# The last output tiles of a two-branch attention kernel: opened ahead on TensorE, closed in two halves, read out by two engines

## The chip, the cores and the metric

The kernel runs on one core of a Trainium2 chip. The metric is the time of one execution in microseconds on the device; of three runs of the kernel before, the median is 965.25 us (964.43 to 966.57). The engines are called as in the profile: PE (matmuls), PEld (its weight loads), DVE and ACT (vector and scalar engine), POOL, and SP, which here only issues transfers. PSUM, where PE writes its results, has eight banks of 128 x 512 f32.

## The reference

Two attention branches share one input x (2048 x 640, bf16) and are mixed by a gate per row:

```python
g = _sigmoid((x * gate_w).sum(-1, keepdims=True))
a = _A_ref(x, A_wqkv, A_wo)      # 32 heads of 20, full softmax attention over 2048 keys
b = _B_ref(x, B_wqkv, B_wo)      # 32 heads of 20, 8 keys at distances 0, 2, ..., 14 back
return g * a + (1 - g) * b
```

Each branch projects x to q, k, v, takes softmax(q k / sqrt(20)) v for each head, and multiplies the heads' results by its own 640 x 640 output matrix (wo).

## The kernel before, in words

**Groups and steps.** Branch A's queries are cut into four chunks of 512 (`QCN`), its heads into eight sets of four (`NQUAD`). One chunk with one set is a group; there are 32, and the chunk is the outer loop. A group has 64 units (16 key blocks x 4 heads). A unit is a score matmul into one PSUM bank, an exponential, and a P·V matmul into bank 5 (`OB`), where each of the four heads has its own 32 partitions. The units are taken in steps of three and two in turn: even steps use banks 0, 1, 2, odd steps banks 3, 4. There are 819 steps, 0 to 818 (`NS`); the last has three units. `mk_qk` (L1061) issues a step's scores, `mk_exp` (L1076) its exponential on ACT into one of six buffers, `mk_pv` (L1084) its P·V matmuls, for several steps together.

**The order.** There is no dynamic scheduling on the chip: the Python program writes one list of instructions per engine, and each engine runs its list in order, waiting on semaphores that `_Sched` derives from the buffers which a task reads and writes. The main loop over steps issues the exponential of step s, then the scores of step s + 2, then whatever side work a small planner finds room for. Side work is written as generators ("lanes": `gen_k`, `gen_q`, `gen_F`, ...), which yield what they need next: `("pe", cost, ...)` for PE time, `("dw", time, cost, ...)` for the DVE work that frees a bank. The planner compares these costs with its own clocks (`lim_pe`, `lim_dve`) and holds a lane back until the step has room for it. Banks 6 and 7 belong to the side work (`take`, `give`). Where there is none, fillers are put on PE (`idle_mm`): into bank 6 or 7 when one is free (L1200), otherwise multiplications by zero added to bank 5 (L1204).

**After a group.** `do_norm` (L629) transposes bank 5 into `rg`, and `gen_norm` takes the reciprocal of the sums (L637), multiplies it by the gate (L638), scales (L643) and transposes back into a slot of `oTn` (L646). All five are on DVE.

**Output.** For a chunk of 512 rows, the output is eight tiles of 128 rows x 320 columns (four blocks `blk`, two halves `hf`). A tile is the sum of 5 matmuls with branch B's result (`b_mm`) and 8 with branch A's (`a_mm`, one per set of heads). `gen_fold` does this for chunks 0 to 2 once the chunk's eight groups are done.

The last chunk is different, since its last group ends with the program. `gen_prefold` computes, while the last two groups run, each tile's sum of B's five matmuls and A's first six (`NPF`), and DVE copies it as f32 into `accin` (L696), which lies in the old weights `WqkB`. After the last P·V matmul, `last_fold` multiplies by the sets six and seven (L708): first eight matmuls of set six, one per tile, into all eight banks, then, after the last group's norm, eight of set seven. DVE then adds `accin` to each bank, tile by tile (L715), into `outl`. After two tiles a block of 128 rows is complete, and a transfer of 160 KB takes it out (L718), on SP and ACT in turn.

Of the kernel before, what the change touches and what calls it, by code (L numbers as in the profile page):

```python
# [5 lines left out]
FP32 = mybir.dt.float32  # L6
# [226 lines left out]
def _build(ctx, nc, A_x, A_wqkv, A_wo, B_wqkv, B_wo, gate_w, out):  # L233
# [69 lines left out]
    lgt = [WqkA[:, 2 + i, D:D + 512] for i in range(2)]  # L303
    repp = [[WqkA[:, 0, D:D + 512], WqkA[:, 1, D:D + 512]], [WkP[i][:, 0:4, :].rearrange("p c k -> p (c k)") for i in range(2)]]
    rep_dead = [[("WkA", 1)], [("WkP", 0), ("WkP", 1)]]
    accin = WqkB[:, :, :].rearrange("p c k -> p (c k)").bitcast(FP32)[:, 0:4 * D].rearrange("p (b k) -> p b k", b=4)
    outl = WvB[:, :, :].rearrange("p c k -> p (c k)")[:, 0:4 * D].rearrange("p (b k) -> p b k", b=4)

    x_v = A_x[0].rearrange("(b p) d -> p b d", p=P)
# [5 lines left out]
    def fap(t, first, dims):  # L315
        return bass.AP(tensor=t, offset=first.offset, ap=[[first.ap[0][0], P]] + dims)
# [123 lines left out]
    def give(b, evac):  # L440
        held[b] = False
        if cur[0] is not None:
            cur[0].hold -= 1
        free_at[b] = evac.fin + 56.0
# [182 lines left out]
    def do_norm(gi):  # L627
        i = gi % 2
        return T("dve", lambda e: e.transpose(rg[i][:, :], bank[OB]), reads=[("ob", j) for j in range(4)],  # L629
                 writes=["rg"], cost=720)  # L630

    def gen_norm(gi):
        qc, q = divmod(gi, NQUAD)
        i = gi % 2
        sl = gi % NOT
        yield ("dve", 420.0, 0.0)
        T("dve", lambda e: e.reciprocal(rr[i][:, :], rg[i][:, 0:512:32]), reads=["rg"], writes=[("rr", i)], cost=240)  # L637
        T("dve", lambda e: e.tensor_tensor(rr[i][:, :], rr[i][:, :], gA[:, 16 * qc:16 * qc + 16], ALU.mult),  # L638
          reads=["gA"], writes=[("rr", i)], cost=180)
        rg_v = fap(rg[i], rg[i][:, 1:2], [[32, 16], [1, DH]])  # L640
        rr_b = fap(rr[i], rr[i][:, 0:1], [[1, 16], [0, DH]])
        yield ("dve", 500.0, 0.0)
        T("dve", lambda e: e.tensor_tensor(rgn[i][:, :, 1:1 + DH], rg_v, rr_b, ALU.mult),  # L643
          reads=["rg", ("rr", i)], writes=["rgn"], cost=500)
        yield ("dve", 710.0, 0.0)
        T("dve", lambda e: e.transpose(oTn[:, sl, :], rgn[i][:, :, :]), reads=["rgn"], writes=[("oTn", sl)], cost=710)  # L646
        normdone[gi] = True
# [8 lines left out]
    def a_mm(o, qc, q, blk, c0):  # L656
        return (o, oTn[:, (qc * NQUAD + q) % NOT, blk * P:(blk + 1) * P], woA_r[:, q, c0:c0 + FW])
# [4 lines left out]
    def a_rd(qc, qs):  # L662
        return [("oTn", (qc * NQUAD + q) % NOT) for q in qs] + [("woA_r", q) for q in qs]
# [20 lines left out]
    def gen_prefold(qc):  # L684

        while not bdone.get(qc) or not all(normdone.get(qc * NQUAD + q) for q in range(NPF)):
            yield ("poll",)
        for blk in range(4):
            for hf in range(2):
                c0 = FW * hf  # L690
                b = yield from take()
                o = bank[b][:, 0:FW]
                mms = [b_mm(o, blk, c0, dp) for dp in range(CN)] + [a_mm(o, qc, q, blk, c0) for q in range(NPF)]
                t = yield from chain(b, mms, b_rd(blk) + a_rd(qc, range(NPF)), cost=140.0)
                yield ("dw", t.fin, 490.0, 0.0)
                give(b, T("dve", lambda e, b=b, blk=blk, c0=c0: e.tensor_copy(accin[:, blk, c0:c0 + FW], bank[b][:, 0:FW]),  # L696
                          reads=[("bk", b)], writes=[("accin", blk, hf), "WqkB"], cost=420))

    def last_fold(qc):
        bs = (0, 1, 2, 3, 4, 6, 7, OB)  # L700
        for q in range(NPF, NQUAD):
            for blk in range(4):
                for hf in range(2):
                    c0 = FW * hf
                    b = bs[2 * blk + hf]
                    o = bank[b][:, 0:FW]
                    wr = [("bk", b)] + ([("ob", j) for j in range(4)] if b == OB else [])
                    T("pe", lambda e, o=o, blk=blk, c0=c0, q=q: e.matmul(o, *a_mm(o, qc, q, blk, c0)[1:], start=(q == NPF),  # L708
                                                                        stop=(q == NQUAD - 1)),
                      reads=a_rd(qc, [q]), **({"writes": wr} if q == NPF else {"accum": wr}), cost=140)  # L710
        for blk in range(4):
            for hf in range(2):
                c0 = FW * hf
                b = bs[2 * blk + hf]
                T("dve", lambda e, b=b, blk=blk, c0=c0: e.tensor_tensor(outl[:, blk, c0:c0 + FW], bank[b][:, 0:FW],  # L715
                                                                  accin[:, blk, c0:c0 + FW], ALU.add),
                  reads=[("bk", b), ("accin", blk, hf)], writes=[("outl", blk), "WvB"], cost=460)
            T("sp" if blk % 2 == 0 else "act", lambda e, blk=blk: e.dma_start(out_v[:, 4 * qc + blk, :], outl[:, blk, :]),  # L718
              reads=[("outl", blk)], writes=[("outd", qc, blk)], dma=True)


    L_flat = fap(L_sb, L_sb[:, 0, 0:1], [[1, 1024]])
# [290 lines left out]
    for h in range(2):  # L1013
        b = QH[h]

        def fn(e, h=h, b=b):
            ins = None
            for j in range(4):
                r = slice(32 * j, 32 * j + 32)
                ins = e.matmul(bank[b][32 * j:32 * j + 1, 0:256], KM[r, 0:1], qabs[r, 256 * h:256 * h + 256], start=False, stop=True,  # L1020
                               skip_group_check=True)
            return ins
# [78 lines left out]
    def lane(gen, name, s0, s1, total, pos=None):  # L1101
        g = _Lane(gen, name, s0, s1, total)
        if pos is None:
            lanes.append(g)
        else:
            lanes.insert(pos, g)
        return g
# [64 lines left out]
    def force(g, s, until=None):  # L1172
        forcing[0] += 1
        n = 0
        while not g.done and not (until is not None and until()):
            if not ready(g, s, INF, INF):
                for o in lanes:
                    if o is not g and not o.done and (o.hold or n > 300):
                        ready(o, s, INF, INF)
            n += 1  # L1180
            assert n < 200000, g.name
        forcing[0] -= 1
# [56 lines left out]
    for s in range(NS):  # L1239
# [49 lines left out]
        def flush(must, old_only=False):  # L1289
            while pend:  # L1290
                s0, i0, un0 = pend[0]
                g0 = un0[0:2]
                if old_only and g0 != (qc, q):
                    return
                obk = sch.bufs[("ob", 0)]
                if un0[2] == 0 and not must and obk[1]:
                    if max(t.fin for t in obk[1]) > clk["pe"] + 150.0:
                        return
                part = []
                while pend and pend[0][0] == s0 and pend[0][2][0:2] == g0:  # L1300
                    _, i1, un1 = pend.pop(0)
                    part.append((i1, un1))
                for (_, un1) in part:
                    key = (un1[1], un1[2] // 3)
                    if key not in vdone:
                        late.append((s, "v") + key)
                        force(vl[un1[1] // 2], s, lambda key=key: key in vdone)

                n0, npv[0] = npv[0], npv[0] + len(part)
                mk_pv(s0, part, (SWITCH if n0 == 0 else 0.0) + MM * (-(-npv[0] // 4) + (-n0 // 4)))  # L1310
                block[0] = False
                if part[-1][1][2] == KBN - 1 and part[-1][1][3] == 3:
                    g1 = g0[0] * NQUAD + g0[1]
                    if g1 == 0 and not vl[0].done:
                        late.append((s, "gate", 0))
                        force(vl[0], s)
                    if g1 >= NOT and not folddone.get((g1 - NOT) // NQUAD):
                        fl = foldl[(g1 - NOT) // NQUAD]
                        late.append((s, "fold", fl.name))
                        force(fl, s)  # L1320
                    do_norm(g1)
                    lane(gen_norm(g1), "norm%d" % g1, s, s + 1, 1.0, 0)

        if gend:
            flush(False, True)
# [29 lines left out]
        if pend and pend[0][0] <= s - NEB + 2:  # L1355
            flush(True)
        pair_side = (pair_side + block[1]) if npv[0] == 0 else 0.0
        while pair_side < FILL * min(3, npend) and clk["pe"] + MM + SWITCH <= lim_pe and s < NS - 2 and npv[0] == 0:
            if not idle_mm():
                break  # L1360
            nidle += 1
            pair_side += MM
# [6 lines left out]
    for g in list(lanes):  # L1369
        late.append((NS, g.name, 0))  # L1370
        force(g, NS)
    last_fold(QCN - 1)
    _INFO["late"] = late
    _INFO["prof"] = prof
    _INFO["ends"] = ends
# [36 lines left out]
```

## Time and profile before

| | |
|---|---|
| median of three runs | 965.25 us (964.43 to 966.57) |
| the profiled execution | 965.52 us |
| its span, first to last instruction | 963.7 us |
| granted TensorE clock, mean | 0.997 |
| last exponential starts | 951.43 us |
| last P·V matmuls start | 953.19 us |
| last group's norm, from first to last instruction | 953.63 to 956.11 us |
| eight additions (L715) | 956.52 to 961.18 us |
| output transfers issued | 957.63 to 961.6 us |

The page gives for each engine its busy time and its share of the span, and the chain of work that ended last. A row of the timeline has the start in us from the span's start, the length, the engine, the line of the kernel, the operation, what it wrote from what it read, the shape, and the count of instructions merged into the row; the bracket tells how long the engine was idle before and what released it. A row of the groups has the busy time in us and the mean of one instruction in ns after the bar, then the idle time before the group. Matmuls overlap, so that several in a row take less than their mean times their count.

### The profile page before, as it was taken

How to read it: one execution, taken by the hardware profiler on the slowest of the kernel's cores; microseconds unless marked ns; L12 is line 12 of the kernel's file. 1: busy time of each engine (PE TensorE's matmuls, PEld its weight loads, DVE VectorE, ACT ScalarE, POOL GpSimd, SP SyncE). 2: the span in 40 equal slices, each digit the busy share in tenths (PEclk: the TensorE clock that was granted, in tenths of full speed). 3: DMA queues.
4: the chain of work that ended last, by engine and by line, in shares of the span. 5: the costliest groups of instructions: out<-in, count | busy, mean ns of one | idle time of the engine just before them, and what ended most of it. 6: DMA issues, size and time to landing. Idle time of an engine off the chain costs nothing.

```text
span 963.7 us, 16441 instructions
## 1 busy us (share of the span) xinstructions
PE 881.2 (91%) x6408; PEld 287.5 (30%) x6408; DVE 570.4 (59%) x1047; ACT 941.6 (98%) x839; POOL 3.1 (0%) x7
## 2 busy tenths in 40 slices
PE   8999999998998899999998989999999998999996
PEld 5333333322222222223322222323222233222332
DVE  5585443445424888762557798355789536987222
ACT  5999999999999999999999999999999999999995
POOL 1000000000000000000000000000000000000000
PEclk9999999999999999999999999999999999999999
DMA  9000000000000000000000000000000000000000
GB/s 311 5 1 21 15 1 1 2 21 14 1 1 1 1 1 1 2 1 7 15 8 1 1 1 1 9 7 7 9 1 1 1 9 15 8 1 1 1 2 28
DMA packets 12032, 12.86 MB, mean 13 GB/s; under 512 B 3380, under 2 KB 11316, under 8 KB 11956
## 3 DMA queue, kind: packets, MB, share of 16 engines
q1 hardware_dynamic: 9700, 11.27, 3.7%
q8 instruction: 53, 0.87, 0.4%
q10 hardware_dynamic: 2256, 0.53, 0.3%
q14 instruction: 23, 0.19, 0.1%
HBM read 9.18 MB, written 2.62 MB: 12 GB/s over the span
## 4 chain that ended last, share of the span: by engine, by line
ACT 73%; issue 17%; PE 8%; DVE 1%; DMA 1%; SPq 0%; DVEq 0%; ACTq 0%
ACT ebuf L1076 72%; PE ps L1061 2%; PE ps L1200 2%; PE ps L386 1%; PE ps L1084 1%; DMA x_tm<-in_A_x_dram 1%; DVE WvB L715 0%; ACT L_sb L838 0%; PE ps L934 0%; DVE Kmax L965 0%; DVE rg L629 0%; DVE oTn L646 0%; PE ps L765 0%; DVE rgn L643 0%; PE ps L865 0%
## 5 line engine op out<-in xcount | busy, mean ns | idle before, releaser
L1076 ACT ACTIVATE ebuf<-ps 128x1536 bf16<-128x1536 f32 (+1 forms) x819 | 929.5, 1370 | 1.3
L1061 PE MATMUL ps<-qT,kT 32*128 32x512 bf16 x2068 | 322.3, 383 | 58.4 <-ACT ebuf L1076 47.2
L1061 PEld LDWEIGHTS ps<-qT,kT 32*128 32x128 bf16 x2068 | 88.7, 91 | 346.2 <-issue 142.0
L1084 PE MATMUL ps<-ebuf,vA 128*21 128x512 bf16 x2048 | 172.6, 384 | 0.6 <-ACT ebuf L1076 0.6
L1200 PE MATMUL ps<-xT,ident 128*128 128x512 bf16 x366 | 142.0, 389 | 9.7
L895 DVE TENSOR_TENSOR bw<-vB,bw 128x640 f32<-128x640 bf16 x112 | 91.9, 820 | 2.1
L899 DVE TENSOR_TENSOR blkacc<-blkacc,bw 128x640 f32<-128x640 f32 x96 | 79.0, 823 | 2.9
L629 DVE STREAM_TRANSPOSE rg<-ps 128x512 f32<-128x512 f32 x32 | 22.9, 717 | 94.8 <-PE ps L1084 94.8
L781 DVE TENSOR_TENSOR prod<-qk 128x512 bf16<-128x512 bf16 x160 | 57.4, 418 | 20.0 <-PE ps L765 19.8
L1200 PEld LDWEIGHTS ps<-xT,ident 128*128 128x128 bf16 x366 | 35.1, 96 | 98.9 <-PE ps L1200 68.1
L386 PE MATMUL ps<-xT,WqkB 128*128 128x512 bf16 x200 | 64.1, 387 | 0.0
L1084 PEld LDWEIGHTS ps<-ebuf,vA 128*21 128x21 bf16 x2048 | 42.0, 90 | 73.1 <-issue 50.8
L750 DVE CAST qk<-ps 128x512 bf16<-128x512 f32 x40 | 27.5, 688 | 47.9 <-PE ps L386 47.8
L386 PE MATMUL ps<-woA_r,oTn 128*128 128x320 bf16 x240 | 50.6, 302 | 0.0
L386 PE MATMUL ps<-xT,WqP 128*128 128x512 bf16 (+1 forms) x165 | 45.6, 376 | 0.7 <-DVE WqP L368 0.5
L386 PE MATMUL ps<-xT,WkP 128*128 128x512 bf16 (+1 forms) x165 | 45.5, 376 | 0.0
L565 DVE CAST qT<-ps 128x512 bf16<-128x512 f32 x31 | 21.4, 690 | 38.3 <-PE ps L386 38.3
L398 DVE TENSOR_SCALAR kT<-ps,e 128x512 bf16<-128x512 f32 x28 | 21.0, 749 | 36.8 <-PE ps L386 36.7
L582 DVE CAST qT<-ps 128x512 bf16<-128x512 f32 x31 | 21.4, 689 | 22.2 <-PE ps L575 22.1
L386 PE MATMUL ps<-WvA,oBacc 128*128 128x320 bf16 x160 | 33.1, 301 | 0.4 <-PE ps L1061 0.4
L386 PE MATMUL ps<-xT,WvB 128*128 128x512 bf16 x100 | 31.7, 380 | 0.0
L813 DVE CAST vB<-ps 128x512 bf16<-128x512 f32 x20 | 13.7, 686 | 26.9 <-PE ps L386 26.9
(98 smaller groups left out, 473.0 us busy)
## 6 DMA issues: line engine op xcount, KB each, us to landing
x_tm<-in_A_x_dram SPq DMA_DIRECT2D x3, 640.0 KB
out_dram<-outsb SPq DMA_DIRECT2D x12, 160.0 KB
WqkB<-in_B_wqkv_dram SPq DMA_DIRECT2D x1, 1600.0 KB
WqkA<-in_A_wqkv_dram SPq DMA_DIRECT2D x2, 700.0 KB
qk<-in_B_wqkv_dram SPq DMA_DIRECT2D x1, 800.0 KB
woA_r<-in_A_wo_dram SPq DMA_DIRECT2D x32, 25.0 KB
WvA<-in_B_wo_dram SPq DMA_DIRECT2D x5, 160.0 KB
x_tm<-in_A_x_dram SPq DMA_DIRECT2D x2, 320.0 KB
```

The lines of the kernel that those rows point to most:

```text
L386: ins = e.matmul(o, l, r, start=(k0 + k == 0), stop=(k0 + k == n - 1))
L565: T("dve", lambda e: e.tensor_copy(qt[:, :], bank[b]), reads=[("bk", b)], writes=[("qT", gi % NQT)], cost=690)
L582: return T("dve", lambda e: e.tensor_copy(qT[gi % NQT][:, :], bank[b]), reads=[("bk", b)], writes=[("qT", gi % NQT)], cost=690)
L629: return T("dve", lambda e: e.transpose(rg[i][:, :], bank[OB]), reads=[("ob", j) for j in range(4)], writes=["rg"], cost=720)
L750: give(b, T("dve", lambda e, dst=dst, b=b: e.tensor_copy(dst, bank[b]), reads=[("bk", b)], writes=[key], cost=690))
L781: t = T("dve", lambda e, r=r, f=f, off=off: e.tensor_tensor(prod[r][:, :], qB[:, f, :], kB[:, f, off:off + 512], ALU.mult), reads=["qB", " ...
L895: T("dve", lambda e, vv=vv, av=av: e.tensor_tensor(tmpB, vv, av, ALU.mult), reads=[("aT", ai), "vB4"], writes=["tmpB"], cost=822)
L899: T("dve", lambda e: e.tensor_tensor(blkacc[:, :, :], blkacc[:, :, :], tmpB, ALU.add), reads=["tmpB"], writes=["blkacc"], cost=822)
L1061: ins = e.matmul(bank[b0 + i], kT[32 * j:32 * j + 32, q, kb * P:(kb + 1) * P], qT[gi % NQT][32 * j:32 * j + 32, :], start=True, stop=True)
L1076: return T("act", lambda e: e.activation(ebuf[s % NEB][:, 0:512 * n], ps[:, b0 * 512:(b0 + n) * 512], ACTF.Exp, scale=SCALE), reads=[("bk" ...
L1084: ins = e.matmul(bank[OB][32 * j:32 * j + DH + 1, :], vA[:, q, kb, VW * j:VW * j + DH + 1], ebuf[s % NEB][:, i * 512:(i + 1) * 512], start ...
L1200: T("pe", lambda e: e.matmul(bank[b], ident[:, :], xT[:, 0, 0:512], start=True, stop=True), reads=["xT", "ident"], writes=[("bk", b)], cos ...
```

## The change

The last chunk's eight tiles are no longer summed by DVE.

- `gen_prefold` leaves each sum made ahead as two bf16 parts: `hi`, a copy, and `lo`, the sum minus `hi`. The lane's allowance for DVE goes from 490 to 1,000 ns.
- `tail_open` opens a tile on PE with three matmuls: set six, and the two parts multiplied by the identity matrix. Tiles 0 and 1 are opened at step 814 in banks 6 and 7 (any side work left over is forced out first, and the two banks are then kept); tiles 2 and 3, in banks 3 and 4, ahead of the last step's P·V matmuls; tiles 4, 5, 6, in banks 0, 1, 2, right after these; tile 7, in bank 5, after the first half has been closed.
- `tail_norm` does the last group's norm in two halves of 256 query rows, each with the five DVE instructions of before, at half their width.
- `tail_close` adds set seven to four tiles and reads them out: the first four on ACT, the last four on DVE and ACT in turn. Three blocks go out on SP and the last on ACT.

```diff
-    accin = WqkB[:, :, :].rearrange("p c k -> p (c k)").bitcast(FP32)[:, 0:4 * D].rearrange("p (b k) -> p b k", b=4)
+    acch = [WqkB[:, :, :].rearrange("p c k -> p (c k)")[:, 4 * D * i:4 * D * i + 4 * D].rearrange("p (b k) -> p b k", b=4)
+            for i in range(2)]
...
-                yield ("dw", t.fin, 490.0, 0.0)
-                give(b, T("dve", lambda e, b=b, blk=blk, c0=c0: e.tensor_copy(accin[:, blk, c0:c0 + FW], bank[b][:, 0:FW]),
-                          reads=[("bk", b)], writes=[("accin", blk, hf), "WqkB"], cost=420))
+                yield ("dw", t.fin, 1000.0, 0.0)
+                hi, lo = [acch[i][:, blk, c0:c0 + FW] for i in range(2)]
+                T("dve", lambda e, o=o, hi=hi: e.tensor_copy(hi, o), reads=[("bk", b)], writes=[("acc", blk, hf), "WqkB"], cost=460)
+                give(b, T("dve", lambda e, o=o, hi=hi, lo=lo: e.tensor_tensor(lo, o, hi, ALU.subtract), reads=[("bk", b), ("acc", blk, hf)],
+                          writes=[("accl", blk, hf)], cost=500))
-    def last_fold(qc):
...
+    TAIL = (6, 7, 3, 4, 0, 1, 2, OB)
...
+    def tail_open(ks):
+        qc, q = QCN - 1, NPF
+        for k in ks:
+            b, blk, c0, o = tail_tile(k)
+            srcs = [a_mm(o, qc, q, blk, c0)] + [(o, ident[:, :], acch[i][:, blk, c0:c0 + FW]) for i in range(2)]
...
+    def tail_norm(h):
...
+        cs, ts = slice(256 * h, 256 * h + 256), slice(8 * h, 8 * h + 8)
+        T("dve", lambda e: e.transpose(rg[i][:, cs], bank[OB][:, cs]), reads=[("ob", j) for j in range(4)], writes=["rg"], cost=360)
...
+        T("dve", lambda e: e.transpose(oTn[:, sl, cs], rgn[i][:, ts, :]), reads=["rgn"],
+          writes=[("oTnh", h)] + ([("oTn", sl)] if h == 0 else []), cost=360)
+    def tail_close(ks, engs):
...
+            T("pe", lambda e, m=a_mm(o, qc, q, blk, c0): e.matmul(*m, start=False, stop=True),
+              reads=[("oTnh", k // 4), ("woA_r", q)],
+              accum=[("bk", b)], cost=140)
+        for k, eng in zip(ks, engs):
...
+                T("act", lambda e, o=o, dst=dst: e.activation(dst, o, ACTF.Copy), reads=[("bk", b)], writes=[("outl", k)], cost=450)
...
+                T("dve", lambda e, o=o, dst=dst: e.tensor_copy(dst, o), reads=[("bk", b)], writes=[("outl", k)], cost=460)
+        for blk in (ks[0] // 2, ks[0] // 2 + 1):
+            T("act" if blk == 3 else "sp", lambda e, blk=blk: e.dma_start(out_v[:, 4 * qc + blk, :], outl[:, blk, :]),
+              reads=[("outl", 2 * blk), ("outl", 2 * blk + 1)], writes=[("outd", qc, blk)], dma=True)
+    def last_fold():
+        tail_open((4, 5, 6))
+        tail_norm(0)
+        tail_norm(1)
+        tail_close((0, 1, 2, 3), ("act",) * 4)
+        tail_open((7,))
+        tail_close((4, 5, 6, 7), ("dve", "act", "dve", "act"))
...
+                if s0 == NS - 1:
+                    tail_open((2, 3))
...
-                    do_norm(g1)
-                    lane(gen_norm(g1), "norm%d" % g1, s, s + 1, 1.0, 0)
+                    if g1 < QCN * NQUAD - 1:
+                        do_norm(g1)
+                        lane(gen_norm(g1), "norm%d" % g1, s, s + 1, 1.0, 0)
...
+        if s == NS - 5:
+            for g in lanes:
+                late.append((s, g.name, 0))
+                force(g, s)
+            held[6] = held[7] = True
+            clk["pe"] += SWITCH
+            tail_open((0, 1))
+            pair_side += 4 * MM
```

More of the change, by code (lines that the diff above doesn't have):

```diff
@@ L694, in gen_prefold @@
                 t = yield from chain(b, mms, b_rd(blk) + a_rd(qc, range(NPF)), cost=140.0)
-                yield ("dw", t.fin, 490.0, 0.0)
-                give(b, T("dve", lambda e, b=b, blk=blk, c0=c0: e.tensor_copy(accin[:, blk, c0:c0 + FW], bank[b][:, 0:FW]),
-                          reads=[("bk", b)], writes=[("accin", blk, hf), "WqkB"], cost=420))
-    def last_fold(qc):
[L700 to L719, printed above, removed]
@@ new lines, in tail_tile, with fn @@
+    def tail_tile(k):
+        blk, hf = divmod(k, 2)
+        c0 = FW * hf
+        return TAIL[k], blk, c0, bank[TAIL[k]][:, 0:FW]
+    def tail_open(ks):
[3 more added lines that the diff above has]
+            srcs = [a_mm(o, qc, q, blk, c0)] + [(o, ident[:, :], acch[i][:, blk, c0:c0 + FW]) for i in range(2)]
+            def fn(e, srcs=srcs):
+                ins = None
+                for n, m in enumerate(srcs):
+                    ins = e.matmul(*m, start=(n == 0), stop=False)
+                return ins
+            wr = [("bk", b)] + ([("ob", j) for j in range(4)] if b == OB else [])
+            T("pe", fn, reads=a_rd(qc, [q]) + [("acc", blk, k % 2), ("accl", blk, k % 2), "ident"], writes=wr, cost=400)
@@ new lines, in tail_norm @@
+    def tail_norm(h):
+        gi = QCN * NQUAD - 1
+        i, sl, qc = gi % 2, gi % NOT, QCN - 1
+        cs, ts = slice(256 * h, 256 * h + 256), slice(8 * h, 8 * h + 8)
+        T("dve", lambda e: e.transpose(rg[i][:, cs], bank[OB][:, cs]), reads=[("ob", j) for j in range(4)], writes=["rg"], cost=360)
+        T("dve", lambda e: e.reciprocal(rr[i][:, ts], rg[i][:, 256 * h:256 * h + 256:32]), reads=["rg"], writes=[("rr", i)], cost=200)
+        T("dve", lambda e: e.tensor_tensor(rr[i][:, ts], rr[i][:, ts], gA[:, 16 * qc + 8 * h:16 * qc + 8 * h + 8], ALU.mult),
+          reads=["gA"], writes=[("rr", i)], cost=180)
+        rg_v = fap(rg[i], rg[i][:, 256 * h + 1:256 * h + 2], [[32, 8], [1, DH]])
+        rr_b = fap(rr[i], rr[i][:, 8 * h:8 * h + 1], [[1, 8], [0, DH]])
+        T("dve", lambda e: e.tensor_tensor(rgn[i][:, ts, 1:1 + DH], rg_v, rr_b, ALU.mult), reads=["rg", ("rr", i)], writes=["rgn"],
+          cost=280)
+        T("dve", lambda e: e.transpose(oTn[:, sl, cs], rgn[i][:, ts, :]), reads=["rgn"],
+          writes=[("oTnh", h)] + ([("oTn", sl)] if h == 0 else []), cost=360)
@@ new lines, in tail_close @@
+    def tail_close(ks, engs):
+        qc, q = QCN - 1, NQUAD - 1
+        for k in ks:
+            b, blk, c0, o = tail_tile(k)
+            T("pe", lambda e, m=a_mm(o, qc, q, blk, c0): e.matmul(*m, start=False, stop=True),
+              reads=[("oTnh", k // 4), ("woA_r", q)],
+              accum=[("bk", b)], cost=140)
+        for k, eng in zip(ks, engs):
+            b, blk, c0, o = tail_tile(k)
+            dst = outl[:, blk, c0:c0 + FW]
+            if eng == "act":
+                T("act", lambda e, o=o, dst=dst: e.activation(dst, o, ACTF.Copy), reads=[("bk", b)], writes=[("outl", k)], cost=450)
+            else:
+                T("dve", lambda e, o=o, dst=dst: e.tensor_copy(dst, o), reads=[("bk", b)], writes=[("outl", k)], cost=460)
+        for blk in (ks[0] // 2, ks[0] // 2 + 1):
+            T("act" if blk == 3 else "sp", lambda e, blk=blk: e.dma_start(out_v[:, 4 * qc + blk, :], outl[:, blk, :]),
+              reads=[("outl", 2 * blk), ("outl", 2 * blk + 1)], writes=[("outd", qc, blk)], dma=True)
@@ L1371, in _build @@
         force(g, NS)
-    last_fold(QCN - 1)
+    last_fold()
     _INFO["late"] = late
```

## The prediction

> **What bounds the kernel now.** I read the page's busy times and chain first, then the last 14 us in order of time, then the groups by form for prices, then the waits.
>
> ```profile
> PE 881.2 (91%) x6408; PEld 287.5 (30%) x6408; DVE 570.4 (59%) x1047; ACT 941.6 (98%) x839; POOL 3.1 (0%) x7
> ACT 73%; issue 17%; PE 8%; DVE 1%; DMA 1%; SPq 0%; DVEq 0%; ACTq 0%
> ```
>
> ACT (the exponentials) is busy 98% of the span, so until 953 us only what delays an exponential counts. After the last one the end is a serial tail:
>
> ```profile
> 948.99 0.84 PE L1200 MATMUL ps<-xT,ident 128*128 128x512 bf16 x2
> 949.77 0.39 PE L1061 MATMUL ps<-qT,kT 32*128 32x512 bf16 x2
> 950.09 0.82 PE L1084 MATMUL ps<-ebuf,vA 128*21 128x512 bf16 x10
> 950.93 0.39 PE L1061 MATMUL ps<-qT,kT 32*128 32x512 bf16 x3
> 951.25 0.84 PE L1200 MATMUL ps<-xT,ident 128*128 128x512 bf16 x2
> 952.02 0.60 PE L1084 MATMUL ps<-ebuf,vA 128*21 128x512 bf16 x5
> 953.19 0.39 PE L1084 MATMUL ps<-ebuf,vA 128*21 128x512 bf16 x3 [0.56 <-ACT ebuf L1076]
> 953.51 1.27 PE L708 MATMUL ps<-woA_r,oTn 128*128 128x320 bf16 x8
> 953.63 0.72 DVE L629 STREAM_TRANSPOSE rg<-ps 128x512 f32<-128x512 f32 x1 [13.97 <-PE ps L1084]
> 954.38 0.25 DVE L637 RECIPROCAL rr<-rg 128x16 f32<-128x16 f32 x1
> 954.67 0.17 DVE L638 TENSOR_TENSOR rr<-rr,gA 128x16 f32<-128x16 f32 x1
> 954.88 0.49 DVE L643 TENSOR_TENSOR rgn<-rg,rr 128x320 bf16<-128x320 f32 x1
> 955.40 0.71 DVE L646 STREAM_TRANSPOSE oTn<-rgn 128x512 bf16<-128x512 bf16 x1
> 956.17 1.26 PE L708 MATMUL ps<-woA_r,oTn 128*128 128x320 bf16 x8 [1.39 <-DVE oTn L646]
> 956.52 4.66 DVE L715 TENSOR_TENSOR WvB<-ps,WqkB 128x320 bf16<-128x320 f32 x8 [0.41 <-PE ps L708]
> ```
>
> The reader sees five DVE instructions in a row (953.63 to 956.11), eight matmuls, then eight DVE additions, one per 0.60 us, while ACT does nothing. The last addition ends at 961.18, the last output transfer is issued there, and the span ends at 963.7, 2.5 us later. Those 4.66 us are what the change attacks.
>
> ```profile
> L1027 DVE CAST qT<-ps 128x256 bf16<-128x256 f32 x1 | 0.4, 425 | 0.4 <-PE ps L1020 0.4
> L990 DVE CAST qT<-ps 128x512 bf16<-128x512 f32 x1 | 0.7, 681 | 0.0
> L1029 ACT ACTIVATE qT<-ps 128x256 bf16<-128x256 f32 x1 | 0.4, 383 | 0.0
> L489 ACT ACTIVATE vA<-ps 128x480 bf16<-128x480 f32 x1 | 0.6, 573 | 0.1
> L696 DVE COPY WqkB<-ps x8: 450/490/492, 907.5 to 939.2; 128x320 f32<-128x320 f32 x8
> ```
>
> These are prices: halving a DVE read from PSUM leaves 0.62 of its time (a fixed 0.17 us and 1.0 ns an element); ACT reads the same 128x256 in 383 ns. The last line is the sums made ahead: eight copies, one per 4.53 us.
>
> **The change part by part.**
>
> *Sums ahead in two bf16 parts.* Eight f32 copies become eight bf16 copies (the 128x320 cast of L676 takes 484 ns) and eight subtractions (nearest row L715, same shape, 492). DVE gets 8 x 0.5 = 4 us more between 907 and 940, where it is busy 0.5 to 2.6 us in each 5 us: hidden, cost 0. What waits on it is the bank handed back, and the planner starts the next tile only after a 1,000 ns allowance instead of 490; a tile takes 11 matmuls, 4+4+3 in three of every four steps. I keep 4.5 us a tile; the limit is in the rivals. Without the cover each tile costs 0.5 us.
>
> *Two tiles opened at step 814* (banks 6 and 7). Six matmuls stand where two fillers stood (948.99 to 949.77). A 128x320 matmul follows the last one by 0.138 us (L708: eight in 1.27, the first 0.30), and four of them are followed by the next kind after 0.64, so 0.09 for the switch: 6 x 0.138 + 0.09 = 0.92 against 0.78. The scores at 949.77 come 0.14 later, the ten matmuls end at about 950.98 and the scores of the last step start there instead of 950.93. Exponential 818 starts 0.50 after them: 0.05 late.
>
> *Fillers of step 816.* Banks 6 and 7 are held, so the fillers go to bank 5, in the form of L1204. The trace's two of those in a row started 0.22 apart (126.58, 0.61 for both), while L1200's each wait for the one before (0.45 apart). They end near 951.83 instead of 952.02: a gain of 0.2.
>
> *Two tiles opened at step 818* (banks 3 and 4). Six more matmuls in front of the last three P·V matmuls on PE, 0.92 us. The five before them start near 951.85 (exponential 817 ends at 951.67) and take 0.54 (two waves of 0.22 and a switch of 0.1), so the six end at 953.31; exponential 818 lets the three go at 953.24. They start about 953.34, 0.15 later than now. Ends: 0, if PE is free sooner, to 0.45, if the fillers keep 0.77 and the 0.14 passes through.
>
> *Norm in halves.* No row shows halves. By fixed part and slope: transpose 0.45, reciprocal 0.20 (from 128x16 246 and 128x128 948), product 0.17, scaling 0.33, transpose 0.44, and 0.13 of gaps as now: 1.72 each, 3.46 for both against 2.48 whole: 0.98 more. Ends: halves at half price (1.31 each: 0.82 less than that) and transposes that cost as much halved as whole (1.06 more). The casts are the nearest rows, so I take 3.46. The transposes of the first half start 0.44 after the three matmuls: 953.78; the first half ends at 955.50, the second at 957.24.
>
> *Nine more opening matmuls after the three, then three more for bank 5.* 9 x 0.138 = 1.24, done at 955.0, before 955.50. The last three wait for the second half's first transpose (955.97) and are done by 956.6, before 957.24. Cost 0. If they were late, each costs 0.14.
>
> *First close and four ACT reads.* The matmuls start at 955.57, ACT 0.35 later (L708 to L715; for ACT 0.2 to 0.5). A 128x320 read lies between 383 and 573: 0.44, four end near 957.6. ACT's next read is possible at 957.80, so they are hidden, with 0.2 to spare.
>
> *Second close, reads shared.* Matmuls 0.07 after 957.24: 957.31. DVE reads from 957.66 to 958.14 and from 958.25 (0.60 apart as L715) to 958.74. ACT: 957.80 to 958.24, 958.15 to 958.59. The block on the ACT queue is issued after 958.74, where it was after 961.18: **2.44 us sooner**.
>
> *Output transfers.* Four of 160 KB, three on SP and one on ACT instead of two each, at about 956.9, 957.7, 958.2, 958.8. A transfer keeps the DMA engines busy for about half a microsecond (share 0.88 in 958.5 to 959.0), so the last two, now 1.2 us apart, still fit 0.5 apart; SP's three issues take 0.33 each and have nothing behind them, and behind ACT's issue nothing is queued. The 2.5 us after the last read stay. Ends: 0 to 0.5 more if they overlap.
>
> A rule against the sharing: the Trainium skill, "ScalarE: Activation LUTs", "Rules for kernel authors", says to use VectorE for simple operations, which is up to about three times faster in bf16. The row says otherwise for reads of PSUM: 383 on ACT, 425 on DVE. By the rule a read would take an estimated 1.45 us, six on ACT would end near 964.6, and the change would lose 3.4 us; by the row it gains 2.44.
>
> **Sum.** The profiled execution took 965.52 (span 963.7 and 1.82 around it), 0.27 over the median of the three runs. 965.52 - 2.44 = 963.08; against the median, **962.8**.
>
> **The rivals.**
>
> *Cheap halves.* The DVE chain costs half for half: 0.82 less, 962.0. For it: these are short instructions with a fixed part that I took from other operations. Against: 681 to 425.
>
> *The gain partly eaten.* PE 0.45 late instead of 0.15 (0.3), and the last transfers overlap (0.5): 963.6; with dear half transposes alone, 963.9. For it: PE has no gap from 949 to 952.6, and all of it is in order. Against: bank 5's fillers give 0.2 back.
>
> *Sharing that doesn't happen.* If ACT and DVE held each other up at PSUM, four last reads at 0.60 would end at 960.0: 964.1. For it: no row shows both on PSUM with nothing else to do. Against: they read different banks, and the eight copies of L696 (0.49 each, 907 to 939) ran beside exponentials that read other banks, with ACT busy 40.00 us of the 40 from 900 to 940.
>
> *Slower: sums ahead too late.* At step 814 the kernel forces whatever is left of them on PE in front of its opening matmuls. The last copy is at 939.2 now; it must be done near 949, so a tile may take 5.9 us instead of 4.53. Each tile left costs 11 x 0.138 = 1.5 us of PE, and the last one's bank comes back 1.4 us later (0.35 and two DVE instructions of 0.49 and hand-overs). ACT's stock covers about 0.2. One tile: 2.7, which eats the gain (965.5); two tiles: 2.7 + 1.5 + 1.4 = 5.6, 968.4. It decides from two tiles, a period of some 6.8 us. For it: twice the allowance before a bank is given. Against: 11 matmuls fit three steps of four with the fourth as allowance.
>
> **How the numbers follow.** Forecast 0.57 (own range 962.1 to 963.3), cheap halves 0.12, partly eaten 0.17, no sharing 0.07, slower 0.07. A measurement of this kernel can tell about 0.2% (1.9 us; the three runs span 2.1). Below 963.3 lie the first two: 0.69; within 0.2% the next two: 0.24; slower 0.07. The range 961.7 to 964.4 takes in both ends of the halves and no sharing, and leaves out the slower case and the edges.
>
> **What the profile after would show.** A first DVE transpose of 128x256 at 953.7 to 954.0 of about 450 ns; ACT copies of 440 ns from 955.9; the last read before 959; a span near 961.3; no ACT idle between 905 and 953; the last sum's subtraction before 945; bank-5 fillers at 951.3. I am wrong if ACT shows a gap near 950, if half transposes take over 600 ns, or if the time from the last read to the end exceeds 2.5 us.

## The result, and the profile after

The changed kernel takes 961.66 us (median of seven runs, 961.59 to 962.67), the kernel before 965.25 us (seven runs, 964.38 to 966.57). The ratio is 0.9967 (95% interval 0.9955 to 0.9978): 3.6 us faster, where 2.4 had been forecast. The profiled execution took 961.62 us, its span is 959.8 us.

The page's busy times, and the chain that ended last by engine:

```profile
PE 860.9 (90%) x6317; PEld 288.6 (30%) x6418; DVE 572.2 (60%) x1054; ACT 943.2 (98%) x845; POOL 3.1 (0%) x7
ACT 73%; issue 17%; PE 8%; DMA 1%; DVE 1%; SPq 0%; ACTq 0%
```

Nothing has moved in the large. ACT has six more instructions (the reads at the end), DVE 2 us more work. PE's count can't be compared: this trace has 6317 matmuls to 6418 weight loads, where the trace of before has 6408 of each, so some of its matmul records are missing, and PE's 20 us less say nothing. The end, in order of time (start, length, engine, line, operation):

```profile
950.28 0.60 PE L1250 MATMUL ps<-ident,zt 128*128 128x512 bf16 x2
950.82 0.60 PE L1130 MATMUL ps<-ebuf,vA 128*21 128x512 bf16 x5
951.35 0.31 PE L719 MATMUL ps<-woA_r,oTn 128*128 128x320 bf16 x1
...
952.27 0.39 PE L1130 MATMUL ps<-ebuf,vA 128*21 128x512 bf16 x3
...
952.71 0.45 DVE L730 STREAM_TRANSPOSE rg<-ps 128x256 f32<-128x256 f32 x1 [12.09 <-PE ps L1130]
...
953.99 0.45 DVE L738 STREAM_TRANSPOSE oTn<-rgn 128x256 bf16<-128x256 bf16 x1
954.36 0.41 DVE L730 STREAM_TRANSPOSE rg<-ps 128x256 f32<-128x256 f32 x1
...
954.49 0.72 PE L745 MATMUL ps<-woA_r,oTn 128*128 128x320 bf16 x4 [0.50 <-DVE oTn L738]
...
954.84 1.43 ACT L752 ACTIVATE WvB<-ps 128x320 bf16<-128x320 f32 x4 [2.77 <-PE ps L745]
...
955.60 0.45 DVE L738 STREAM_TRANSPOSE oTn<-rgn 128x256 bf16<-128x256 bf16 x1
955.63 1.80 SPq L756 DMA_DIRECT2D out_dram<-WvB  x3
...
956.10 0.72 PE L745 MATMUL ps<-woA_r,oTn 128*128 128x320 bf16 x4 [0.49 <-DVE oTn L738]
956.45 0.89 DVE L754 CAST WvB<-ps 128x320 bf16<-128x320 f32 x2 [0.40 <-PE ps L745]
956.59 0.77 ACT L752 ACTIVATE WvB<-ps 128x320 bf16<-128x320 f32 x2 [0.32 <-PE ps L745]
957.43 0.37 ACTq L756 DMA_DIRECT2D out_dram<-WvB  x1
```

Where eight additions took 4.66 us after the norm, two reads on each of two engines now take 0.89 and 0.77 us; the first four lie beside the norm's second half. From the last P·V matmuls to the end it is 959.8 - 952.27 = 7.5 us instead of 963.7 - 953.19 = 10.5.

**Where the 3.6 us came from.** The changed kernel's last exponential starts at 950.45 us of its trace, that of before at 951.43. The programs hardly differ up to there, so this 0.98 needs an explanation of its own. Counted from the first exponential (19.51 before, 19.32 after), the last one starts 931.92 us later before and 931.13 after: 0.19 of the 0.98 lies ahead of the first exponential, where the inputs land, and 0.79 between. The windows of the kernel before, then of the kernel after (us of the stretch, busy time of PE, PEld, DVE, ACT, POOL with their counts, clock, DMA share, GB/s), show where:

```profile
308.00:313.00 5.00, 4.68 (x28) 1.02 (x29) 2.07 (x3) 4.81 (x5) 0.00 (x0) 0.66 0.00 0
```

```profile
308.00:313.00 5.00, 4.22 (x32) 1.17 (x32) 3.13 (x6) 5.00 (x6) 0.00 (x0) 1.00 0.00 0
```

In the execution of before, TensorE's clock was halved for 3.4 us from 308.9 us on; PE got fewer matmuls done and ACT ran dry (4.81 of 5.00 us busy). Set beside e4 below, which is the kernel before up to the additions and whose profile shows the full clock there, the exponentials of before keep step up to 309 us, fall 1.07 us behind between 310.6 and 318.0, and stay 0.9 behind from 332.8 on. That isn't the change's doing: the clock dropped at the same place in one of the runs of an edited changed kernel below (f1, clock 0.66 in the same window, 932.00 us from first to last exponential), and in no other profile of this study. The part of a profile that belongs to the change is therefore measured from the last exponential's start to the end of the span (in us, from the trace's own times; each ratio is to runs of the kernel before made beside that kernel's):

| kernel | last exponential to last read's end | to the end of the span | median us (runs) | ratio to before (95%) |
|---|---|---|---|---|
| before | 9.75 | 12.28 | 965.25 (7) | |
| after | 6.90 | 9.37 | 961.66 (7) | 0.9967 (0.9955 to 0.9978) |
| after, once more | 6.90 | 9.37 | 962.53 (5) | 0.9968 (0.9956 to 0.9981) |
| e1: last reads on DVE alone | 8.76 | 11.09 | 964.38 (11) | 0.9987 (0.9978 to 0.9996) |
| e2: norm whole | 6.84 | 9.53 | 962.91 (11) | 0.9976 (0.9967 to 0.9985) |
| e3: nothing opened ahead | 7.28 | 9.86 | 963.24 (10) | 0.9976 (0.9967 to 0.9985) |
| e4: before, additions unchained | 8.37 | 10.89 | 964.13 (11) | 0.9988 (0.9979 to 0.9996) |
| f1: one bf16 part | 6.76 | 9.22 | 962.65 (6) | 0.9972 (0.9961 to 0.9983) |
| f3: one tile ahead | 6.76 | 9.22 | 962.09 (6) | 0.9965 (0.9953 to 0.9977) |
| f3, once more | 6.76 | 9.21 | 962.32 (7) | 0.9969 (0.9958 to 0.9980) |
| f4: f3, norm's front whole | 6.83 | 9.29 | 961.80 (5) | 0.9965 (0.9952 to 0.9977) |
| f5: the same, all opened early | 6.33 | 9.06 | 962.43 (7) | 0.9973 (0.9962 to 0.9984) |

The change's own gain is 12.28 - 9.37 = 2.9 us in the tail, less 0.1, since its last exponential starts 931.13 us after the first one, against 931.04 in e4 (whose clock did not drop). That exponential is also 0.09 us shorter (1.62 against 1.71), and it ends 932.75 us after the first one in both. Counted from its end to the end of the span, before takes 10.58 us, e4 9.18, e1 9.48 and the changed kernel 7.75, so 2.83 us are the change's. The other 0.8 of the medians' 3.6 is how the runs fell: the times of each kernel lie in groups some 0.9 us apart (four of the changed kernel's seven at 961.6 to 961.7, three at 962.5 to 962.7; before, two at 964.4, four at 965.2 to 965.6, one at 966.6), and a median of few runs goes by how many fall in each. The lowest times agree with the tail: 964.38 and 961.59, 2.8 apart. Where a program was profiled twice, the tail repeats to 0.01 us, so the experiments are read by the tail first.

### The profile page after: what moved, and what is told of

Same layout as the page of the kernel before. It is cut to its first block, busy times and chain, and to the rows that moved or that the text cites. A ratio compares the mean times of both kernels' runs of the same rounds, so it can differ in the third digit from the quotient of the medians.

```text
span 959.8 us, 16367 instructions
## 1 busy us (share of the span) xinstructions
PE 860.9 (90%) x6317; PEld 288.6 (30%) x6418; DVE 572.2 (60%) x1054; ACT 943.2 (98%) x845; POOL 3.1 (0%) x7
## 3 DMA queue, kind: packets, MB, share of 16 engines
HBM read 9.18 MB, written 2.62 MB: 12 GB/s over the span
## 4 chain that ended last, share of the span: by engine, by line
ACT 73%; issue 17%; PE 8%; DMA 1%; DVE 1%; SPq 0%; ACTq 0%
ACT ebuf L1122 73%; PE ps L1107 3%; PE ps L1246 2%; PE ps L387 1%; PE ps L1130 1%; DMA x_tm<-in_A_x_dram 1%; ACT L_sb L884 0%; PE ps L980 0%; PE ps L719 0%; DVE Kmax L1011 0%; PE ps L811 0%; PE ps L576 0%; PE ps L911 0%; DVE oTn L738 0%; SPq L325 0%
## 5 line engine op out<-in xcount | busy, mean ns | idle before, releaser
L1246 PE MATMUL ps<-xT,ident 128*128 128x512 bf16 x316 | 122.7, 389 | 16.1 <-PE ps L1107 6.3
L387 PE MATMUL ps<-xT,WqkB 128*128 128x512 bf16 x179 | 58.2, 384 | 2.2 <-PE ps L1107 1.4
L387 PE MATMUL ps<-xT,WqP 128*128 128x512 bf16 (+1 forms) x154 | 43.3, 375 | 1.5 <-issue 0.6
L387 PE MATMUL ps<-xT,WkP 128*128 128x512 bf16 (+1 forms) x151 | 42.6, 375 | 1.9 <-issue 1.1
L470 PE MATMUL ps<-WvA,xT 128*128 128x160 bf16 (+1 forms) x320 | 29.5, 233 | 0.0
```

The source lines that it names most:

```text
L387: ins = e.matmul(o, l, r, start=(k0 + k == 0), stop=(k0 + k == n - 1))
L470: ins = e.matmul(bank[b][:, i_ * wn:(i_ + 1) * wn], xT[:, c, kb * P:(kb + 1) * P], WvA[:, c, w0:w0 + wn], start=(c == 0), stop=(c == CN - 1))
L1246: T("pe", lambda e: e.matmul(bank[b], ident[:, :], xT[:, 0, 0:512], start=True, stop=True), reads=["xT", "ident"], writes=[("bk", b)], cos ...
```

## The experiments

**e1: the sharing of the reads.** All eight last reads on DVE.

```diff
-        tail_close((0, 1, 2, 3), ("act",) * 4)
+        tail_close((0, 1, 2, 3), ("dve",) * 4)
...
-        tail_close((4, 5, 6, 7), ("dve", "act", "dve", "act"))
+        tail_close((4, 5, 6, 7), ("dve",) * 4)
```

> The changed kernel with all eight last reads on DVE, none on ACT. Theory (the gain over before is the sharing of the reads): DVE is busy with both norm halves until about 956.05, so all eight reads queue behind them, 8 x 0.45 us from 956.45 to 960.0 where the last read now ends at 957.36: 2.6 us slower than the changed kernel, so nearly as slow as before. Rival (the gain is that PE does the adding, and a read of one source is cheap wherever it runs): under 1 us slower than the changed kernel.

Measured: 11.09 us from the last exponential to the end, 1.7 more than after; the last read 1.86 later. So neither number. The line of its timeline tells why the theory's 2.6 was too much:

```profile
955.98 3.24 DVE L754 CAST WvB<-ps 128x320 bf16<-128x320 f32 x8
```

The eight reads begin at once after the norm, since the first four tiles have been closed by then, and one starts every 0.40 us, not every 0.45. Sharing the reads with ACT is worth 1.7 us. But the rival has its point too: with DVE reading alone, what was 4.66 us of additions is 3.24 us of reads. Why reads should be so much cheaper than additions of the same shape is what e4 asks.

**e2: the halves.** The norm in one piece, the reads shared from its end.

```diff
-    def tail_norm(h):
+    def tail_norm(h, n=2):
...
-        cs, ts = slice(256 * h, 256 * h + 256), slice(8 * h, 8 * h + 8)
+        cs, ts = slice(256 * h, 256 * h + 256 * n), slice(8 * h, 8 * h + 8 * n)
...
-        tail_norm(1)
-        tail_close((0, 1, 2, 3), ("act",) * 4)
         tail_open((7,))
+        tail_close((0, 1, 2, 3), ("dve", "act", "dve", "act"))
```

> The changed kernel with the last group's norm in one piece and the eight reads shared from its end. Theory (the halves carry little): norm 2.48 us instead of 3.34 in two, so the closes start near 955.25, four reads on each engine end near 957.4 where now they end at 957.36: within 0.2 us of the changed kernel. Rival (the halves carry the gain, since ACT reads four tiles beside the second half): 0.9 us or more slower, four reads of 0.36 to 0.45 us coming after the norm that now lie beside it, less what the shorter norm gives.

Measured: 9.53 us, 0.16 more than after, as the theory had it. The last read even ends 0.06 sooner, but 2.69 us instead of 2.46 pass from there to the end: all four blocks become ready within 1.1 us, and their transfers run back to back (e2's windows; last two columns the share of the DMA engines and GB/s):

```profile
957.50:958.00 0.50, 0.00 (x0) 0.00 (x0) 0.17 (x1) 0.05 (x1) 0.00 (x0) 1.00 0.93 323
958.00:958.50 0.50, 0.00 (x0) 0.00 (x0) 0.00 (x0) 0.00 (x0) 0.00 (x0) 1.00 0.98 330
958.50:959.00 0.50, 0.00 (x0) 0.00 (x0) 0.00 (x0) 0.00 (x0) 0.00 (x0) 0.64 1.02 351
959.00:959.50 0.50, 0.00 (x0) 0.00 (x0) 0.00 (x0) 0.00 (x0) 0.00 (x0) 0.50 0.86 297
```

Halving the norm is thus worth 0.2 us, and only by sending the first two blocks earlier.

**e3: opening ahead.** No tile is opened before the last P·V matmuls.

```diff
-                if s0 == NS - 1:
-                    tail_open((2, 3))
...
-            tail_open((0, 1))
-            pair_side += 4 * MM
...
-        tail_open((4, 5, 6))
+        tail_open((0, 1, 2, 3, 4, 5, 6))
```

> The changed kernel with no tile opened ahead of the last P.V matmuls: tiles 0 to 6 all opened after them. Theory (opening ahead hides little): the last P.V matmuls start 0.15 us sooner, 21 opening matmuls at 0.138 us end 0.85 us after the first half of the norm, but the second half's closes come only 0.35 us late; the end is 0.1 to 0.3 us later than in the changed kernel. Rival (opening ahead is needed): the first close's delay passes on to the end, 0.9 us slower or more.

Measured: 9.86 us, 0.5 more than after: between the two. The chain that ended last goes through PE and then ACT, not through DVE's norm:

```profile
952.69 2.96 PE ps L719 x21
955.65 0.15 PE ps L745
955.80 0.02 issue
955.83 2.08 ACT WvB L752 x6
```

The first closes come 0.8 us late, as expected, and ACT's six reads then run without a pause (2.08 us): the delay does reach the end. It is shortened to 0.4, since in the changed kernel ACT needs 2.52 us for the six, with a pause of 0.32 before the last two. The theory had looked at DVE's reads alone.

**e4: the additions of before, unchained.** The kernel before, with one edit: the eight additions no longer all name the buffer `WvB`, nor each two of them the same block, so the program lets none wait for the one before it.

```diff
-                  reads=[("bk", b), ("accin", blk, hf)], writes=[("outl", blk), "WvB"], cost=460)
+                  reads=[("bk", b), ("accin", blk, hf)], writes=[("outl", blk, hf)] + (["WvB"] if blk + hf == 0 else []), cost=460)
...
-              reads=[("outl", blk)], writes=[("outd", qc, blk)], dma=True)
+              reads=[("outl", blk, 0), ("outl", blk, 1)], writes=[("outd", qc, blk)], dma=True)
```

> The kernel before, with one edit: the eight last additions no longer name one common buffer, so that none waits for the one before it. Theory (the 0.60 us from one addition to the next is 0.49 of work and 0.11 of waiting for its own engine, which the changed kernel's reads, 0.41 to 0.45 apart, don't do): 7 x 0.15 = 1.0 us faster than before. Rival (0.60 is the price of an addition from two sources): no change.

Measured: 10.89 us, 1.39 less than before and more than the 1.0 expected; the median is 964.13 us, ratio 0.9988 (0.9979 to 0.9996). The group of the additions, and their row in order of time:

```profile
L715 DVE TENSOR_TENSOR WvB<-ps,WqkB 128x320 bf16<-128x320 f32 x8 | 3.3, 481 | 0.4 <-PE ps L708 0.4
```

```profile
955.65 3.28 DVE L715 TENSOR_TENSOR WvB<-ps,WqkB 128x320 bf16<-128x320 f32 x8 [0.40 <-PE ps L708]
```

Eight in 3.28 us instead of 4.66: one every 0.40 us. The 0.60 us of before were 0.40 of work and 0.20 of waiting for DVE itself. In the chain of before this wait stands between any two additions, as three short lines that are easily passed over; here is one stretch of it:

```profile
959.50 0.50 DVE WvB L715
960.00 0.03 issue
960.03 0.02 DVEq L173
960.05 0.04 issue
960.10 0.50 DVE WvB L715
```

So almost half of the change's 2.83 us was to be had from the kernel before by renaming a buffer, with no second engine, no halves and no bf16 parts. Without the wait an addition is as quick as a read, eight in 3.28 us against e1's 3.24, and with one engine reading, adding on PE gains nothing over adding on DVE: counted from the last exponential's end, e1 takes 0.3 us more than e4 (though e1 also has the longer norm in halves). What PE's adding brings is that only copies are left to do, of which ACT takes six. So the 2.83 us are 1.39 for the wait (before to e4), less 0.29 from e4 to e1, and 1.73 for ACT's share of the reads (e1 to after).

**The changed kernel once more**, for more of its times.

> The changed kernel once more, unedited, beside the next three, to have more of its times. Theory (of its 3.6 us over before by medians about 2.8 come from the tail, the rest from how the runs fell before the last step: times of both kernels lie in groups some 0.9 us apart, 964.4 and 965.3 before, 961.6 and 962.6 after): from last exponential to end 9.4 us again, lowest time 2.8 us under the lowest of before. Rival (all 3.6 us are the change's): lowest time 3.6 us under the lowest of before.

Measured: 9.37 us from the last exponential to the end, the lowest time 961.80 us against 964.66 of before, 2.9 apart: the theory. In its profiled execution the first exponential started at 20.29 us instead of 19.32, and that execution took 962.59 us: the 0.97 are ahead of anything the change touches.

**f1: one bf16 part.** The second part of the sums is left out, with its subtraction and its matmul, so the sums made ahead are rounded to bf16; the lane's allowance for DVE is 490 again.

```diff
-                yield ("dw", t.fin, 1000.0, 0.0)
+                yield ("dw", t.fin, 490.0, 0.0)
...
-            srcs = [a_mm(o, qc, q, blk, c0)] + [(o, ident[:, :], acch[i][:, blk, c0:c0 + FW]) for i in range(2)]
+            srcs = [a_mm(o, qc, q, blk, c0)] + [(o, ident[:, :], acch[i][:, blk, c0:c0 + FW]) for i in range(1)]
...
```

> The changed kernel with one bf16 part per sum: the second part, its subtraction on DVE and its matmul are left out (so the sums made ahead are rounded to bf16), and the allowance is 490 again. Theory (the second part is hidden, but for two of its matmuls in front of the last P.V matmuls): these start 0.15 us sooner, end to end 0.1 to 0.2 us faster than the changed kernel. Rival (eight subtractions and sixteen more matmuls cost something besides): 0.5 us faster or more.

Measured: 9.22 us, 0.15 less, and the last P·V matmuls 1.68 us after the last exponential's start instead of 1.82: the theory. The second part costs what its two matmuls ahead of the last P·V matmuls cost, and nothing else that a profile shows.

**f3: one tile ahead.** Tile 3 is opened after the last P·V matmuls, tile 6 after the first closes.

```diff
-                    tail_open((2, 3))
+                    tail_open((2,))
...
-        tail_open((4, 5, 6))
+        tail_open((3, 4, 5))
...
-        tail_open((7,))
+        tail_open((6, 7))
```

> The changed kernel with one tile instead of two opened ahead of the last P.V matmuls; tiles 3, 4, 5 after them, 6 and 7 after the first closes. Theory (two tiles make PE 0.15 us late, and there are 0.6 us of idle PE before the first closes): last P.V matmuls at the exponential's end again, 0.15 us faster than the changed kernel. Rival (the end is set by the transfers, which run back to back from 958.0 to 958.9, not by the last read): no faster, since the last two transfers only start as soon as the engines are free.

> The run with one tile ahead once more, beside the other. Theory: 9.2 us from the last exponential's start to the end again, lowest time 0.1 to 0.2 us under the lowest of the changed kernel. Rival (its gain was chance): the changed kernel's 9.35 to 9.39.

Measured: 9.22 and 9.21 us, 0.15 to 0.17 less than the changed kernel; the P·V matmuls again 1.68 us after the exponential's start, released by it. The theory. The times don't settle so small a gain (lowest 961.61 and 961.74; the changed kernel 961.59 and 961.80).

**f4: the front of the norm whole.** First transpose, reciprocal and product in one piece, scaling and second transpose in halves; one of the first four reads on DVE; and f3's edit.

```diff
...
+        if h == 0:
+            T("dve", lambda e: e.transpose(rg[i][:, :], bank[OB]), reads=[("ob", j) for j in range(4)], writes=["rg"], cost=720)
...
-        tail_close((0, 1, 2, 3), ("act",) * 4)
+        tail_close((0, 1, 2, 3), ("act", "act", "act", "dve"))
...
```

> As the run with one tile ahead, and the first transpose, the reciprocal and the product of the norm whole, only scaling and second transpose in halves; the fourth read goes to DVE. Theory (the last read sets the end): norm 2.9 us instead of 3.34, last read 0.35 us sooner, 0.5 us faster than the changed kernel together with the 0.15. Rival (the transfers set the end): the first half is 0.36 us later, so the first transfer starts later, four of them run back to back, and the end moves by less than 0.2 us.

Measured: 9.29 us, no better than f3; but it doesn't tell theory and rival apart, because a third cause came in. The norm ends 0.59 us sooner than in the changed kernel, and the second closes don't follow it: they start at 956.48, straight after six opening matmuls, with PE not idle.

```profile
956.21 0.43 PE L719 MATMUL ps<-WqkB,ident 128*128 128x320 bf16 x2
956.25 1.55 SPq L757 DMA_DIRECT2D out_dram<-WvB  x3
956.48 0.71 PE L746 MATMUL ps<-woA_r,oTn 128*128 128x320 bf16 x4
```

**f5: the same, with all tiles opened before the first closes** (the lines shown are against the changed kernel).

```diff
-        tail_open((4, 5, 6))
+        tail_open((3, 4, 5, 6))
         tail_norm(0)
+        tail_open((7,))
...
```

> The run before with both edits had its second closes held up by six opening matmuls on PE. Here all tiles are opened before the first closes (tile 2 ahead, 3 to 6 after the last P.V matmuls, 7 after the whole first transpose). Theory (the last read sets the end, 2.45 us before it in every run so far with room between transfers): last read 6.45 us after the last exponential's start, end at 8.9, 0.45 us faster than the changed kernel. Rival (the transfers set it): first issue 5.4 us after that start, 0.95 to the first bytes, four transfers of 0.5 us back to back, 0.9 to the end: 9.2 to 9.25, 0.1 to 0.15 us faster than the changed kernel.

Measured: the last read ends 6.33 us after the exponential's start, 0.57 sooner than in the changed kernel, but the end comes at 9.06, 0.31 sooner. So the answer lies between: the reads are no longer what sets the end alone, and 2.74 us instead of 2.46 pass from the last read to the end. f5's windows show all four transfers in one run:

```profile
957.50:958.00 0.50, 0.00 (x0) 0.00 (x0) 0.02 (x1) 0.04 (x1) 0.00 (x0) 1.00 0.96 330
958.00:958.50 0.50, 0.00 (x0) 0.00 (x0) 0.00 (x0) 0.00 (x0) 0.00 (x0) 1.00 0.98 330
958.50:959.00 0.50, 0.00 (x0) 0.00 (x0) 0.00 (x0) 0.00 (x0) 0.00 (x0) 0.73 1.05 361
959.00:959.50 0.50, 0.00 (x0) 0.00 (x0) 0.00 (x0) 0.00 (x0) 0.00 (x0) 0.50 0.70 241
```

The DMA engines are full from 957.5 to past 959, at some 330 to 360 GB/s, and at that rate the four blocks of 160 KB take an estimated 1.9 us. By its profile f5 is the fastest of all, 0.3 us under the changed kernel; its times (lowest 961.41, median 962.43) don't tell it from the others.

## Why the prediction was right, and where its sizes were off

The direction and the mechanism were right; the median, 961.66, lies 0.04 us below the low end of the range. By that number alone the rival of cheap halves (962.0) lies nearer than the forecast (962.8). That is chance: the steps below show that the halves were not cheap, and 0.8 of the gain is not the change's. The step sizes, against the trace, with the 0.98 us taken off by which the two traces are apart at the last exponential:

- *Sums ahead in two parts, cost 0.* Right. The casts come one per 4.7 us (906.40 to 939.60; 4.5 had been kept), the last subtraction is done at 940.6, ACT is busy for 40.00 of the 40 us from 900 to 940 and 10.00 of the next 10. So the slower rival, sums made too late for step 814, did not come near: 5.9 us a tile were allowed.
- *Six opening matmuls at step 814, 0.92 us.* Measured 0.92 (947.93 to 948.85).
- *Fillers to bank 5, done in 0.53.* Measured 0.53 (950.28 to 950.81).
- *Last P·V matmuls 0.15 late.* Measured: 932.96 us after the first exponential's start, against 932.81 in e4, which up to there is the kernel before: 0.15. f3 shows its cause, since with three opening matmuls instead of six there it is gone.
- *Norm in halves, 3.46 us.* Measured 3.34 (952.71 to 956.05). The prices of the five instructions were right to 0.02 (0.45, 0.20, 0.17, 0.33, 0.45); but the second half's first transpose starts at 954.36, before the first half's last one ends at 954.44. The rival of cheap halves falls: half a transpose costs 0.45, not 0.36.
- *Four ACT reads hidden, 0.44 each.* Measured 440 ns, one every 0.33, done at 956.27, where ACT's next read starts at 956.59.
- *Second close to last read, 1.43 us.* This step failed in size: measured 1.26. "0.60 apart as L715" took the distance of the additions as the price of a read; it held 0.20 of waiting that the reads don't have (e4). They start 0.41 apart. With that, DVE and ACT end together, at 957.34 and 957.36.
- *2.5 us from the last read to the end.* Measured 2.46. The last two transfers run back to back (share 1.00 in 958.0 to 958.5) without costing anything yet.

Forecast for the tail: 2.44 sooner. Measured: 2.83; the norm gives 0.12, the reads 0.17 and the end 0.07 more than was thought. The remaining 0.8 of the medians' 3.6 was no step of the prediction. In the profiled pair what is left lies ahead of the last exponential (0.19 in the landing of the inputs and 0.79 with the drop of the clock); where it lies in the other runs isn't shown.

The reading of the old profile was wrong in one point that matters more than its 0.17 us. It called the 4.66 us of additions what the change attacks, as if this were their price; 1.38 of these were a wait of DVE for itself. e4 shows that without it the kernel before ends 1.39 us sooner, and the change as it stands ends 1.44 us sooner than that (counted from the last exponential's end).

The sharing was weighed against a rule of the Trainium skill. The rule ("ScalarE: Activation LUTs", "Rules for kernel authors": operations like add and mul on VectorE, up to about three times faster in bf16) does not carry over to copies of f32 from PSUM: 440 ns on ACT, 484 on DVE, one every 0.33 and 0.40 us.

## What to carry to other kernels

Where an engine does the same instruction several times at the end of a program, compare the distance from start to start with the length of one: 0.60 against 0.49 us here meant a wait for the engine itself, made by a buffer name that all of them shared, and renaming it was worth almost half of what a much larger change brought. Give a serial tail's reads to an engine that has run out of work, but count the transfers behind them: in e2 and f5 the four blocks became ready within 1.1 us, and 0.2 to 0.3 us more passed from the last read to the end. And where two traces are compared, line them up at the last common instruction before the change: a quarter of the apparent gain in this pair of traces (1.0 of 3.9 us) came before it.

## What the runs showed of the hardware

- DVE instructions without a wait between them start before the one in front has ended: 128x320 additions of 481 ns each one every 0.40 us, reads one every 0.40; with a wait for the one in front, one every 0.60 (492 ns each). The Trainium skill says in "VectorE: DVE Perf Modes", section "The DRAIN you can't avoid", that a semaphore after each of eight copies cost nothing extra. Here a wait for it cost 0.20 us at each of seven additions, and the measurement decides.
- TensorE's clock was halved for 3.4 us at 308.5 to 308.9 us in two of the twelve profiled executions, in programs that are the same up to there. PE had not stood still: in the 3.4 us just ahead it was busy for 2.08 us (before) and 2.06 us (f1). That doesn't tell those runs from the others, since f3 once more has 2.08 us in the like stretch and kept the full clock. What sets the drop off in some runs and not in others stays open.
- Writing the output out, the 16 DMA engines moved 330 to 360 GB/s when full, with 160 KB a transfer; 0.8 to 1.0 us pass from the issue to the first bytes, and as much from the last bytes to the end of the span.
